# Attention mixed with a Fourier sublayer on one core: keep-warm transposes, first loads, the copy of the sums and the last stores rearranged

## The chip, the cores and the metric

The kernel runs on one core of one Trainium2 chip. A core has a matrix engine (TensorE; PE in the rows below, its weight loads PEld), a vector engine (VectorE, DVE), an activation engine (ScalarE, ACT), a general one (GpSimd, POOL), a queue engine that issues DMAs (SyncE, SP), and 16 DMA engines that all queues share. The metric is device time in microseconds for one execution; lower is better. The kernel before took 1694.63 us, the median of three runs (1694.62, 1694.63 and 1698.86).

## The reference

With x of 2048 rows and 512 columns, the output is `g * a + (1 - g) * b`, where:

```python
g = sigmoid((x * gate_w).sum(-1, keepdims=True))
# a: attention with 32 heads of 16 columns
qkv = (x @ wqkv).reshape(B, S, 3, H, Dh).transpose(2, 0, 3, 1, 4)
scores = einsum("bhqd,bhkd->bhqk", q, k) * Dh ** -0.5
a = einsum("bhqk,bhkd->bhqd", softmax(scores), v).transpose(0, 2, 1, 3).reshape(B, S, D) @ wo
# b: real part of a Fourier transform over columns, then rows
b = dft_seq_re @ (x @ dft_hid_re.T) - dft_seq_im @ (x @ dft_hid_im.T)
```

Everything is float32.

## The kernel before, in words

**Precision.** A float32 product is made of three passes: each operand is split into a high part (a copy in a shorter format) and a low part (the rest), and high·high, high·low and low·high are summed. So a split is one copy on ACT or POOL and one subtraction on DVE or POOL, and a product over 128 rows of contraction is three matmuls. Matmuls use the array in two halves, 64 rows each (j = 0 and 1), that run beside each other.

**The front** (lines 480 to 615). x arrives transposed in 16 tiles (d = 0..3 for the contraction, c = 0..3 for 512 rows of x each), wqkv in column slices. SP issues these loads in program order (lines 500 to 508): for each d the tile x(d, 0) and 256 columns (`near`) of the q weights, then the `near` columns of the k weights, x(·, 1), the other 256 columns (`far`) of q, x(·, 2), `far` of k, x(·, 3). ACT and DVE split each tile (`split`, lines 381 to 383). PE begins with `NWARM = 32` transposes of the identity matrix into scratch banks (`keep_warm`, line 514), whose results nobody reads. Then `project_t` makes its first products: q for f = 0 (columns 0 to 127) on x(·, 0), k for f = 0, q for f = 1 (columns 128 to 255). In the first product every group of three matmuls belongs to one d, and `fillers` puts six more transposes after each of the first three groups. One product is 12 slots, and work such as later splits is handed out by slot number (`after(n, f)`, line 272). `follow` issues the second half-array pass of a product 17 matmuls later (`LAG`).

**Scores, exponentials, values.** For each pair of heads, `score` (line 711) writes a tile of scores into a PSUM bank, ACT takes the exponential (line 693), `pv` (line 723) multiplies by the values and sums over the keys in one bank, `pvb`. Beside the values `pvb` collects the sums of the exponentials, the divisors of the softmax. After 16 steps of keys `pvb` is complete: `quotients` (line 753) copies it to `ob` (ACT, line 758, in this part of the program), four POOL DMAs gather the sums into `lc` (line 761), and `divide` returns three later steps (reciprocal, spread, scaling), which `staged` hands out by the number of the macro step m. `scan` (line 744 on PE, line 746 on DVE) looks for the maxima of heads to come.

**Blocks.** From m = 90 (`SINGLES`) to m = 234 (`OUTM`) two macro steps form a block, whose order of scores (e), scans (c) and spectral products (s, line 969) is written out in `BLOCK_ORDERS`: 80 entries with 24 spectral products per half (the long block), or 56 with 16 (the short one). Both have 16 score tiles. Scores and scans take turns in five PSUM banks: a bank's next matmul has to wait until ACT or DVE has read it. At the end of a block PE does four `pv` steps in a row (32 matmuls in the profile's rows). Every fourth block follows a completed `pvb`: this concerns 18 of the 20 copies of line 758, 12 ahead of long blocks and 6 ahead of short ones. POOL splits the coefficients of the spectral products (lines 253 and 254), one unit per 12 products.

**The end.** After the last `pv`, the last head pair is divided, and the rows 3, 7 to 15 of the output (in tiles of 128 rows) are finished: row 8 first, then 9, 13, 10, 14, 11, 15 on DVE (`take_in`, line 914), and 12, 3, 7 on POOL (line 1182), after products with g on ACT. SP stores 3 and 7 (`store_out(3)`, line 918), then 8, 9, 10, 11; ACT's queue stores 13, 12, 14, 15 (line 1207). A queue issues in order: a store whose row is not finished holds up those behind it.

Of the kernel before, what the change touches and what calls it, by code (L numbers as in the profile page):

```python
# [18 lines left out]
P = 128  # L19
# [4 lines left out]
NP = H // 2  # L24
NB = S // P
ND = D // P
NC = S // 512
# [7 lines left out]
FRONT = 5 * SCANS + 44  # L35
FOLDED = range(FRONT)
FOLD_PACE = 2.05
NWARM = 32
STEPS = NP * PERIODS
MACROS = STEPS // 2  # L40
LAG = 17
# [1 line left out]
SINGLES = 90  # L43
# [16 lines left out]
def build(tc, x, xT, wqkv, wo, wrT, wiT, cr, ci, gate, out):  # L60
    nc = tc.nc
    with ExitStack() as ctx:
# [197 lines left out]
        with ExitStack() as px:  # L260
# [7 lines left out]
            def scan_bank():  # L268
                singles[0] += 1
                return psf.tile([P, 512], F32, tag=f"s{singles[0] % 5}", name="s")  # L270
# [86 lines left out]
                    close(ps)  # L357

            starts, fillers = set(), []

            def products(parts, close):

                ps = product_bank()
                pairs = [(lhs[a], rhs[b]) for lhs, rhs in parts for a, b in ((0, 0), (0, 1), (1, 0))]
                for n, (lhs, rhs) in enumerate(pairs):
                    nc.tensor.matmul(ps, lhs[0:64], rhs[0:64], start=n == 0, stop=False)  # L366
                    issued[0] += 1
                    if n == len(pairs) - 1:
                        ends[ps.name] = issued[0]
                        starts.add(ps.name)  # L370
                        marks[:] = marks[-8:]
                        if pace[0] is None or seen[0] >= FRONT:
                            seen_by(mark(lhs, rhs))
                    behind_.append((ps, lhs, rhs, n == len(pairs) - 1, close))
                    if len(behind_) > LAG:
                        follow()
                    if n % 3 == 2 and fillers:
                        fillers.pop()(6)
                    beside()

            def split(hi, lo, raw, engine):
# [14 lines left out]
            if True:  # L396
# [88 lines left out]
                    return t[d // 2][:, q4[d % 2]]  # L485

                rq, rk = ([quarter(raws[4 + i], d) for d in range(ND)] for i in range(2))
                near, far = slice(0, 256), slice(256, 512)

                def load_x(c):  # L490
                    for d in range(ND):
                        nc.sync.dma_start(quarter(raws[d], c), xT[d * P:(d + 1) * P, q4[c]])

                def load_cols(i, cols):
                    for h in range(2):
                        src = wqkv[2 * h * P:2 * h * P + 2 * P, 512 * i:512 * i + 512]
                        nc.sync.dma_start(raws[4 + i][h].rearrange("p (d m) -> p d m", m=512)[:, :, cols],
                                          src.rearrange("(d p) m -> p d m", p=P)[:, :, cols])

                for d in range(ND):  # L500
                    nc.sync.dma_start(quarter(raws[d], 0), xT[d * P:(d + 1) * P, q4[0]])
                    nc.sync.dma_start(rq[d][:, near], wqkv[d * P:(d + 1) * P, near])
                load_cols(1, near)
                load_x(1)
                load_cols(0, far)
                load_x(2)
                load_cols(1, far)
                load_x(3)
                nc.sync.dma_start(ones_d.rearrange("a (b c) -> (a b) c", c=32), ones)
                gb = ep.tile([P, D], F32, tag="gb", name="gb", bufs=1)  # L510
                after(40, nc.sync.dma_start, gb, gate.to_broadcast([P, D]))

                warm = [scan_bank(), scan_bank()]
                def keep_warm(k):
                    for n in range(k):
                        nc.tensor.transpose(warm[n % 2][:, 0:P], ident, ident)

                keep_warm(NWARM)
                fillers.extend([keep_warm] * 3)
                for d in range(ND):  # L520
                    split_x(d, 0)
                    split_w(wq, d, rq[d], cols=near)
                for d in range(ND):
                    after(1 + 2 * d, split_w, wk, d, rk[d], nc.vector, near)
                    after(84 + 4 * d, split_w, wq, d, rq[d], nc.vector, far)
                    after(124 + 6 * d, split_w, wk, d, rk[d], nc.vector, far)
                    for c, at in zip(range(1, NC), (10, 32, 56)):
                        after(at + 4 * d, split_x, d, c)
                order = [(wq, q_d, 0, 0), (wk, k_d, 0, 0), (wq, q_d, 1, 0)]
                order += [(w, dst, 0, c) for c in range(1, NC) for w, dst in ((wk, k_d), (wq, q_d))]  # L530
# [89 lines left out]
        with ExitStack() as pa:  # L620
# [98 lines left out]
            def pv(step):  # L719
                p, h, kb = step // PERIODS, step % PERIODS // NB, step % NB  # L720
                banks.step()
                for c, j, r in quads:
                    nc.tensor.matmul(pvb[r:r + VC, :], va[:, kb, 2 * p + j, :], es[step][c][0][:, j * 512:j * 512 + 512],  # L723
                                     start=kb == 0, stop=kb == NB - 1, tile_position=(0, r))
                unused.extend(i for e, i in es.pop(step).values())
                exponentials()
                if kb == NB - 1 and step < STEPS - 1:
                    m = step // 2 + 1
                    for n, f in zip((3, 6, 9) if m < SINGLES else (3, 5, 7) if p < NP - 1 else (2, 3, 4), divide(*quotients(p, h))):
                        staged.setdefault(m + n, []).append(f)  # L730

            scans, late, leaving = [FRONT, FRONT], [], []

# [463 lines left out]
            take_in(8, groups[8][0])  # L1197
            for f in [scaled(8, 1)] + add:
                f()
            store_out(3)  # L1200
            for t in (10, 11):
                part(t, 2)
            for t, j in ((9, 0), (9, 1), (10, 0), (10, 1), (11, 0), (11, 1)):
                take_in(t + 4 * j, groups[t][j])
            for j, queue in enumerate((nc.sync, nc.scalar)):
                for t in (9, 8, 10, 11) if j else (8, 9, 10, 11):
                    queue.dma_start(out[(t + 4 * j) * P:(t + 4 * j + 1) * P, :], ys[t + 4 * j])


# [24 lines left out]
```

## Time and profile before

One execution was profiled. It took 1695.7 us; the span from its first to its last instruction is 1693.9 us.

| engine | busy us | share of the span |
|---|---|---|
| PE | 1676.0 | 99% |
| PE weight loads | 1074.2 | 63% |
| ACT | 1298.4 | 77% |
| DVE | 1256.8 | 74% |
| POOL | 706.9 | 42% |

Of the rows of a timeline: start, duration, engine, line of the kernel, operation, output<-inputs, shapes, number of merged instructions, and in brackets how long the engine was idle before and what ended that. A row with x12 stands for 12 instructions in a row. A matmul's record overlaps with the next one's, so starts tell its rate better than durations do. Stores and loads stand under the queue that issues them; when their bytes moved is read from the DMA rows.

### The profile page before, as it was taken

Reading aid. Unit: us, or ns where it says so; the run is one execution under the profiler, and the core shown is the slowest. Engines: PE = TensorE matmul, PEld = TensorE weight load, DVE = VectorE, ACT = ScalarE, POOL = GpSimd, SP = SyncE. Lnnn points to the kernel's source line nnn. Section 1 sums busy time; section 2 is a strip of 40 time slices with the busy share of each in tenths; the row PEclk is TensorE's granted clock in tenths of the full one; section 3 lists DMA queues with packets and bytes.
Section 4 is the critical chain, followed back from the end, with each engine's and each line's share of the span. In section 5 each row is a group of like instructions: output and inputs, shape, how many; then the busy total and the mean of one; then the engine's idle time right before and its main releaser. Section 6 shows DMA issues by size and latency. Waiting matters only on the chain.

```text
span 1693.9 us, 37082 instructions
## 1 busy us (share of the span) xinstructions
PE 1676.0 (99%) x13688; PEld 1074.2 (63%) x13688; DVE 1256.8 (74%) x2352; ACT 1298.4 (77%) x2427; POOL 706.9 (42%) x890
## 2 busy tenths in 40 slices
PE   9999999999999999999999999999999999999997
PEld 7877778833333333777777677666777777666553
DVE  5699899867777777888888888556888888556324
ACT  5589988799999999656666566777556665778884
POOL 0464301454562322454454444444535445445321
PEclk9999999999999999999999999999999999999999
DMA  7665234554442222233332332573332433335512
GB/s 269 228 231 164 73 113 145 179 179 140 127 139 71 65 69 77 64 109 101 86 100 84 100 101 81 153 246 87 117 107 80 127 89 118 104 107 154 159 34 100
DMA packets 140005, 206.61 MB, mean 122 GB/s; under 512 B 58848, under 2 KB 61392, under 8 KB 139824
## 3 DMA queue, kind: packets, MB, share of 16 engines
q1 hardware_dynamic: 97552, 173.76, 33.2%
q0 software_dynamic: 41696, 29.44, 6.6%
q8 instruction: 108, 1.77, 0.4%
q10 hardware_dynamic: 576, 1.05, 0.2%
q14 instruction: 73, 0.60, 0.1%
HBM read 137.89 MB, written 65.81 MB: 120 GB/s over the span
## 4 chain that ended last, share of the span: by engine, by line
PE 94%; DVE 1%; ACT 1%; DMA 1%; issue 1%; DVEq 0%; ACTq 0%
PE pvb L723 28%; PE z L969 24%; PE s L711 17%; PE s L744 9%; PE xy L350 5%; PE s L187 5%; PE xy L366 5%; DMA q_d<-el 0%; ACT fold L191 0%; DVE y L914 0%; DVE fold L193 0%; DMA ks<-kf_d 0%; ACT c L382 0%; ACT xg L553 0%; DVE rb L1186 0%
## 5 line engine op out<-in xcount | busy, mean ns | idle before, releaser
L693 ACT ACTIVATE e<-s 128x512 f32<-128x512 f32 (+1 forms) x1862 | 1012.5, 681 | 244.2 <-PE s L744 184.6
L746 DVE TENSOR_REDUCE mx<-s 128x1 f32<-128x512 f32 x1320 | 870.3, 688 | 282.7 <-PE s L744 186.2
L711 PE MATMUL s<-qs,ks 50*128 50x512 f32 x2040 | 620.8, 418 | 0.0
L969 PE MATMUL z<-b,chi 64*128 64x512 f32 x2060 | 517.5, 392 | 0.0
L723 PE MATMUL pvb<-e,va 128*17 128x512 f32 x4096 | 492.7, 595 | 0.0
L711 PEld LDWEIGHTS s<-qs,ks 50*128 50x128 f32 x2040 | 306.6, 185 | 210.7 <-ACT e L693 153.1
L744 PE MATMUL s<-ks,qs 48*128 48x512 f32 x1320 | 426.8, 400 | 0.7 <-ACT ab L578 0.7
L969 PE MATMUL z<-b,clo 64*128 64x512 f32 x1030 | 338.6, 393 | 0.0
L969 PEld LDWEIGHTS z<-b,chi 64*128 64x128 f32 x2060 | 327.9, 186 | 13.5
L193 DVE CUSTOM_DVE_ANT_0 fold<-s,fold 128x512 f32<-128x512 f32 x364 | 240.0, 689 | 24.3 <-ACT fold L191 7.6
L744 PEld LDWEIGHTS s<-ks,qs 48*128 48x128 f32 x1320 | 227.4, 185 | 35.8 <-issue 18.7
L723 PEld LDWEIGHTS pvb<-e,va 128*17 128x17 f32 x4096 | 92.3, 96 | 242.3 <-issue 237.5
L187 PE MATMUL s<-ks,qs 48*128 48x512 f32 x728 | 234.4, 400 | 1.5 <-ACT fold L191 1.1
L191 ACT ACTIVATE fold<-s 128x512 f32<-128x512 f32 x364 | 200.5, 605 | 28.5 <-PE s L187 27.3
L969 PEld LDWEIGHTS z<-b,clo 64*128 64x128 f32 x1030 | 175.7, 186 | 8.1 <-POOL clo L254 0.4
L254 POOL TENSOR_TENSOR clo<-craw,chi 128x512 fp32r<-128x512 f32 x126 | 161.8, 1284 | 10.4
L761 POOL DMA_DIRECT2D lc<-ob x124 | 62.5, 510 | 248.2 <-ACT ob L758 156.4
L253 POOL CAST chi<-craw 128x512 fp32r<-128x512 f32 x126 | 77.3, 614 | 212.4 <-PE z L969 166.9
L187 PEld LDWEIGHTS s<-ks,qs 48*128 48x128 f32 x728 | 133.6, 184 | 37.8 <-DVE mx L193 12.3
L366 PE MATMUL xy<-w,b 64*128 64x512 f32 x384 | 120.3, 399 | 0.0
L350 PE MATMUL xy<-w,b 64*128 64x512 f32 x384 | 117.0, 393 | 0.0
L914 DVE SCALAR_TENSOR_TENSOR y<-z,g,y 128x512 f32<-128x512 f32 x44 | 32.5, 750 | 75.1 <-PE z L969 70.0
(137 smaller groups left out, 1519.7 us busy)
## 6 DMA issues: line engine op xcount, KB each, us to landing
craw<-cr SPq DMA_DIRECT2D x64, 256.0 KB
craw<-ci SPq DMA_DIRECT2D x64, 256.0 KB
qs<-q_d SPq DMA_DIRECT2D x126, 128.0 KB
ks<-k_d SPq DMA_DIRECT2D x108, 128.0 KB
ab_d<-ab SPq DMA_DIRECT2D x32, 256.0 KB
y_d<-y SPq DMA_DIRECT2D x32, 256.0 KB
b<-bs_d SPq DMA_DIRECT2D x32, 256.0 KB
qs<-q_d SPq DMA_DIRECT2D x126, 64.0 KB
```

What stands on the lines that cost most here:

```text
L187: nc.tensor.matmul(ps, rows.q[qb // 8][b:b + 48, qb % 8 * P:(qb % 8 + 1) * P], rows.k[c // 2][b:b + 48, c % 2 * 512:(c % 2 + 1) * 512], st ...
L191: seen_by(nc.scalar.activation(fold[j], ps, AF.Relu))
L193: seen_by(nc.vector.tensor_tensor_reduce(out=fold[j], in0=ps, in1=fold[j], scale=1.0, scalar=-3.0e38, op0=ALU.add, op1=ALU.max, accum_out= ...
L254: sub(lo, raw, hi.bitcast(F32))
L350: ins = nc.tensor.matmul(ps, lhs[64:P], rhs[64:P], start=False, stop=last)
L366: nc.tensor.matmul(ps, lhs[0:64], rhs[0:64], start=n == 0, stop=False)
L693: nc.scalar.activation(e if j is None else e[:, j * 512:j * 512 + 512], ps, AF.Exp, scale=SCALE)
L711: nc.tensor.matmul(ps, rows.k[kb // 8][b:b + 50, kb % 8 * P:(kb % 8 + 1) * P], rows.q[h][b:b + 50, c * 512:c * 512 + 512], start=True, sto ...
L723: nc.tensor.matmul(pvb[r:r + VC, :], va[:, kb, 2 * p + j, :], es[step][c][0][:, j * 512:j * 512 + 512], start=kb == 0, stop=kb == NB - 1, ...
L744: nc.tensor.matmul(ps, rows.q[qb // 8][b:b + 48, qb % 8 * P:(qb % 8 + 1) * P], rows.k[c // 2][b:b + 48, c % 2 * 512:(c % 2 + 1) * 512], st ...
L746: nc.vector.tensor_reduce(mx[p][:, j, qb, c:c + 1], ps, axis=AX.X, op=ALU.max)
L969: nc.tensor.matmul(ps, pr_.lhs(j), pr_.rhs(j), start=group.count[j] == 1, stop=group.count[j] == group.size)
```

## The change

Four edits.

1. `NWARM` goes from 32 to 20, and the fillers from 6, 6, 6 to 3, 5, 5 transposes.
2. The first weight loads take 128 columns (`near`) in place of 256. The next 128 columns of q (`middle`) are loaded ahead of x(·, 1) and split from slot 9 on; `far` of q is as before; k's remaining 384 columns (`rest`) are one load per half. The splits of x(·, 1) and x(·, 2) move from slots 10 and 32 to 16 and 34.
3. Inside the blocks the copy of `pvb`, with its four POOL DMAs, is issued at the middle of the next block's order in place of its start.
4. The last stores: SP stores rows 8, 9, 3, 10, 7, 11, ACT's queue 12, 13, 14, 15.

```diff
-NWARM = 32
+NWARM = 20
...
-                        fillers.pop()(6)
+                        keep_warm(fillers.pop(0))
...
-                near, far = slice(0, 256), slice(256, 512)
+                near, middle, far, rest = slice(0, 128), slice(128, 256), slice(256, 512), slice(128, 512)
...
                 load_cols(1, near)
+                load_cols(0, middle)
                 load_x(1)
                 load_cols(0, far)
                 load_x(2)
-                load_cols(1, far)
+                load_cols(1, rest)
                 load_x(3)
...
                 keep_warm(NWARM)
-                fillers.extend([keep_warm] * 3)
+                fillers.extend((3, 5, 5))
...
                     after(1 + 2 * d, split_w, wk, d, rk[d], nc.vector, near)
+                    after(9 + 2 * d, split_w, wq, d, rq[d], nc.vector, middle)
                     after(84 + 4 * d, split_w, wq, d, rq[d], nc.vector, far)
-                    after(124 + 6 * d, split_w, wk, d, rk[d], nc.vector, far)
-                    for c, at in zip(range(1, NC), (10, 32, 56)):
+                    after(124 + 6 * d, split_w, wk, d, rk[d], nc.vector, rest)
+                    for c, at in zip(range(1, NC), (16, 34, 56)):
...
                 if kb == NB - 1 and step < STEPS - 1:
                     m = step // 2 + 1
-                    for n, f in zip((3, 6, 9) if m < SINGLES else (3, 5, 7) if p < NP - 1 else (2, 3, 4), divide(*quotients(p, h))):
-                        staged.setdefault(m + n, []).append(f)
+
+                    def begin():
+                        for n, f in zip((3, 6, 9) if m < SINGLES else (3, 5, 7) if p < NP - 1 else (2, 3, 4),
+                                        divide(*quotients(p, h))):
+                            staged.setdefault(m + n, []).append(f)
+
+                    if SINGLES <= m < OUTM:
+                        staged.setdefault(m + 1, []).append(begin)
+                    else:
+                        begin()
...
-            store_out(3)
             for t in (10, 11):
                 part(t, 2)
...
-            for j, queue in enumerate((nc.sync, nc.scalar)):
-                for t in (9, 8, 10, 11) if j else (8, 9, 10, 11):
-                    queue.dma_start(out[(t + 4 * j) * P:(t + 4 * j + 1) * P, :], ys[t + 4 * j])
+            for queue, rows in ((nc.sync, (8, 9, 3, 10, 7, 11)), (nc.scalar, (12, 13, 14, 15))):
+                for t in rows:
+                    queue.dma_start(out[t * P:(t + 1) * P, :], ys[t])
```

**PE at the start.** Before (s is a scratch bank, xy a product; b and w are the split parts of x and of the q weights):

```order
L516 MATMUL s<-ident 128x128 x32
L366 MATMUL xy<-b_223,w_255 128x512
L366 MATMUL xy<-b_224,w_255 128x512
L366 MATMUL xy<-b_223,w_257 128x512
L516 MATMUL s<-ident 128x128 x6
L366 MATMUL xy<-b_225,w_255 128x512
L366 MATMUL xy<-b_226,w_255 128x512
L366 MATMUL xy<-b_225,w_257 128x512
L516 MATMUL s<-ident 128x128 x6
```

And with the change:

```order
L364 MATMUL s<-ident 128x128 x20
L371 MATMUL xy<-b_225,w_257 128x512
L371 MATMUL xy<-b_226,w_257 128x512
L371 MATMUL xy<-b_225,w_259 128x512
L364 MATMUL s<-ident 128x128 x3
L371 MATMUL xy<-b_227,w_257 128x512
L371 MATMUL xy<-b_228,w_257 128x512
L371 MATMUL xy<-b_227,w_259 128x512
L364 MATMUL s<-ident 128x128 x5
```

The products stand as before; 12 transposes are gone ahead of them and 5 between them.

**ACT at the first block with a copy** (e are exponentials; up to here they come with tiles of 1024 columns among them, from here on in tiles of 512). Before:

```order
L693 ACTIVATE e<-s 128x512 x2
L693 ACTIVATE e<-s_10401 128x1024
L693 ACTIVATE e<-s 128x512 x2
L693 ACTIVATE e<-s_10423 128x1024
L693 ACTIVATE e<-s 128x512 x50
L758 COPY ob<-pvb 128x512
L693 ACTIVATE e<-s 128x512 x64
```

And with the change:

```order
L695 ACTIVATE e<-s 128x512 x2
L695 ACTIVATE e<-s_10394 128x1024
L695 ACTIVATE e<-s 128x512 x2
L695 ACTIVATE e<-s_10416 128x1024
L695 ACTIVATE e<-s 128x512 x60
L768 COPY ob<-pvb 128x512
L695 ACTIVATE e<-s 128x512 x64
```

The copy has moved behind ten more exponentials, that is behind 10 of the 16 of the long block that it stood in front of. In the short blocks it moves behind 7 of 16.

**SP at the end** (one y tile holds two neighbouring rows of the output: y_22353 holds 3, y_23453 holds 7, y_23640 holds 8 and 9, y_23700 holds 10 and 11). Before:

```order
L918 DMA out_dram<-y_22353 128x512
L918 DMA out_dram<-y_23453 128x512
L918 DMA out_dram<-y_22353 128x512
L918 DMA out_dram<-y_23453 128x512
L1207 DMA out_dram<-y_23640 128x512 x2
L1207 DMA out_dram<-y_23700 128x512 x2
```

And with the change, where the same tiles are y_22346, y_23446, y_23633 and y_23693:

```order
L928 DMA out_dram<-y_22346 128x512
L928 DMA out_dram<-y_23446 128x512
L1216 DMA out_dram<-y_23633 128x512 x2
L1216 DMA out_dram<-y_22346 128x512
L1216 DMA out_dram<-y_23693 128x512
L1216 DMA out_dram<-y_23446 128x512
L1216 DMA out_dram<-y_23693 128x512
```

The stores of 8 and 9 now stand ahead of those of 3 and 7, and 10 between these two.

More of the change, by code (lines that the diff above doesn't have):

```diff
@@ L359, in build, with keep_warm @@
             starts, fillers = set(), []
+            warm = [scan_bank(), scan_bank()]
+            def keep_warm(k):
+                for n in range(k):
+                    nc.tensor.transpose(warm[n % 2][:, 0:P], ident, ident)
             def products(parts, close):
@@ L511, in build @@
                 after(40, nc.sync.dma_start, gb, gate.to_broadcast([P, D]))
[L513 to L516, printed above, removed]
                 keep_warm(NWARM)
-                fillers.extend([keep_warm] * 3)
+                fillers.extend((3, 5, 5))
                 for d in range(ND):
```

## The prediction

> **What bounds the kernel now.** I read the chain of waits first, then the timelines of the three places that the change touches: the first 14 us, the blocks with a copy, the last 11 us.
>
> ```profile
> PE 1676.0 (99%) x13688; PEld 1074.2 (63%) x13688; DVE 1256.8 (74%) x2352; ACT 1298.4 (77%) x2427; POOL 706.9 (42%) x890
> PE 94%; DVE 1%; ACT 1%; DMA 1%; issue 1%; DVEq 0%; ACTq 0%
> ```
>
> PE carries the chain from the first transpose to the last product. So time taken out of PE's queue at the start shortens the whole, unless something else sets the pace right behind. A delay on ACT costs only what it makes PE wait. The last microseconds, after PE's last product, belong to the stores. The profiled execution took 1695.7 us, 1.8 above its span of 1693.9 and 1.1 above the median of the runs, 1694.63. The three terms below are differences, worked out inside that span; I take their sum off the median.
>
> **Edit 1 and 2, the front.** PE's timeline, then its weight loads for the transposes in two stretches (count, shortest/median/longest in ns, first and last start):
>
> ```profile
> 1.35 6.50 PE L516 MATMUL s<-ident 128*128 128x128 f32 x32 [1.35 <-POOL ident masks.py:199]
> 7.79 0.96 PE L366 MATMUL xy<-b,w 64*128 64x512 f32 x3
> 8.68 0.88 PE L516 MATMUL s<-ident 128*128 128x128 f32 x6
> 9.48 0.96 PE L366 MATMUL xy<-b,w 64*128 64x512 f32 x3
> ...
> 13.71 0.48 PE L366 MATMUL xy<-b,c 64*128 64x512 f32 x1
> ```
>
> ```profile
> L516 PEld LDWEIGHTS s<-ident x27: 182/226/229, 1.4 to 6.7; 128*128 128x128 f32 x27
> ```
>
> ```profile
> L516 PEld LDWEIGHTS s<-ident x21: 138/140/143, 7.3 to 12.6; 128*128 128x128 f32 x21
> ```
>
> 27 transposes start between 1.4 and 6.7, 0.20 to 0.21 us apart with loads of 226 ns; from 7.3 on the loads take 140 ns, and six transposes in 0.88 us are some 0.11 to 0.12 apart. PE runs at about half rate until 7.1 and at full rate after (the granted clock in the rows of the windows is 1.00 all along; the durations tell it). Between the products a group of six fillers takes 9.48 - 8.68 = 0.80, and three matmuls with their change-over 8.68 - 7.79 = 0.89.
>
> With the change the 20 transposes end at about 1.4 + 20 x 0.213 = 5.7. The first group then runs at half rate until 7.1 and ends near 7.3; three fillers (0.80 - 3 x 0.11 = 0.47) bring the second group to 7.8; with five fillers (0.69) the third stands at 9.4, the fourth at 11.0, and the k product starts at 11.8 in place of 13.71. In short: work before the change of rate is done at half rate whatever it is, so each of the 17 transposes is worth its fast price, 17 x 0.11 = **1.9 us**.
>
> This holds if the operands are there. The last one that each needs, and ACT's long idle stretch behind, read from the timelines of DVE and ACT:
>
> ```profile
> 9.64 0.42 DVE L383 TENSOR_TENSOR w<-raws,w 128x256 fp32r<-128x256 f32 x1
> 10.21 1.45 DVE L383 TENSOR_TENSOR c<-raws,c 128x256 fp32r<-128x256 f32 x4
> ```
>
> ```profile
> 18.00 0.59 ACT L455 CAST eh<-xy 128x512 fp32r<-128x512 f32 x1 [4.16 <-PE xy L350]
> ```
>
> ```profile
> 5.00:10.00 5.00, 5.00 (x28) 4.20 (x27) 3.56 (x8) 3.01 (x7) 0.00 (x0) 1.00 0.99 311
> ...
> 30.00:35.00 5.00, 4.66 (x40) 3.88 (x40) 2.73 (x7) 1.78 (x4) 0.58 (x1) 1.00 0.59 216
> ```
>
> Already before, the fourth q operand is split at 10.06 (needed at 11.0) and the k weights at 11.66 (needed at 11.8). From 5 to 10 us the DMA engines are full (the last two columns: share 0.99, 311 GB/s), so bytes set the arrival. With half the columns, 0.5 of the 2.0 MB ahead of the last k weights go away, 1.6 us at 311 GB/s, and the splits shrink. `middle` adds 0.25 MB ahead of x(·, 1), which still arrives after 2.75 MB in place of 3.0. Its eight small splits (DVE's took 0.36 each for 256 columns, ACT's about as much, so at most 1.5 us on each) fit into ACT's 4.16 us of idleness; without that cover they would hold up `eh`, the copy of the first product, and after it the third product's bank. `rest` is 384 columns in place of 256 for a product that stands far later. Moving the x splits by 2 to 6 slots stays ahead of their products at slots 36 and 60. I put these at nothing. Bounds of the term: 1.0 (one operand 0.9 late) to 2.2 (the gate of PE's rate opens earlier, nothing is late).
>
> **Edit 3, the copy.** PE's `pv` rows mark the ends of blocks, first long blocks, then short ones; below them ACT's rows from the same two places:
>
> ```profile
> 758.60 3.63 PE L723 MATMUL pvb<-e,va 128*17 128x512 f32 x32
> ...
> 771.79 3.63 PE L723 MATMUL pvb<-e,va 128*17 128x512 f32 x32
> ...
> 785.13 3.63 PE L723 MATMUL pvb<-e,va 128*17 128x512 f32 x32
> ```
>
> ```profile
> 1111.55 3.63 PE L723 MATMUL pvb<-e,va 128*17 128x512 f32 x32
> 1121.84 3.63 PE L723 MATMUL pvb<-e,va 128*17 128x512 f32 x32
> 1132.19 3.63 PE L723 MATMUL pvb<-e,va 128*17 128x512 f32 x32
> ```
>
> ```profile
> 775.53 0.59 ACT L758 COPY ob<-pvb 128x512 f32<-128x512 f32 x1 [4.38 <-PE pvb L723]
> 776.02 6.13 ACT L693 ACTIVATE e<-s 128x512 f32<-128x512 f32 x12
> 782.45 2.07 ACT L693 ACTIVATE e<-s 128x512 f32<-128x512 f32 x4 [0.30 <-PE s L711]
> 789.28 6.16 ACT L693 ACTIVATE e<-s 128x512 f32<-128x512 f32 x12 [4.77 <-PE s L744]
> 795.62 2.06 ACT L693 ACTIVATE e<-s 128x512 f32<-128x512 f32 x4 [0.18 <-PE s L711]
> ```
>
> ```profile
> 1115.73 8.02 ACT L693 ACTIVATE e<-s 128x512 f32<-128x512 f32 x16 [2.25 <-PE s L711]
> 1125.65 0.59 ACT L758 COPY ob<-pvb 128x512 f32<-128x512 f32 x1 [1.90 <-issue]
> ```
>
> A long block without a copy takes 771.79 - 758.60 = 13.19, the one with it 13.34: 0.15 more. Short ones take 10.29 and 10.35: 0.06 more. Over 12 long and 6 short blocks that is 12 x 0.15 + 6 x 0.06 = 2.2 us, all that this edit can win. It is so little because the copy sits in ACT's idle time under `pv` (4.38 and 1.90 us); the first exponential is late by less than 0.1.
>
> The new place is not idle. The copy holds ACT for 776.02 - 775.53 = 0.49 us. In a long block it follows ten exponentials of a run of 12 back to back; two more are late by 0.49, then the idle 0.18 takes some of it, and the last four are late by 0.31. In a short block all 16 are back to back, and the nine behind the copy are late by 0.49. What waits is the next matmul in the bank that a late exponential holds, and PE's queue behind it. No row of before shows that wait, so bounds: nothing, if five banks cover it, or 0.49 per copy, if PE is held for all of it. Half of what is late seems nearest, since a bank comes round only after four others, and the last banks of a block are not wanted until `pv`, 3.63 us without scores, is over: 0.15 long, 0.25 short. 12 x 0.15 + 6 x 0.25 = 3.3, less the 2.2 saved: **1.1 us lost**, between 2.2 won and 8.8 - 2.2 = 6.6 lost.
>
> The four DMAs of the copy wait on POOL:
>
> ```profile
> L761 POOL DMA_DIRECT2D lc<-ob x124 | 62.5, 510 | 248.2 <-ACT ob L758 156.4
> ```
>
> They hold POOL for 4 x 0.51 = 2.0 us some 5 us later than now. Behind them stands the split of the next coefficient unit, not wanted before a whole unit (half a long block, 6.6 us) has passed, and the reciprocal is two macro steps away; I put that at nothing. If it were not covered, the spectral product itself would start up to 2.0 late.
>
> **Edit 4, the end.** DVE and POOL finish the rows, SP and ACT's queue store them, then the DMA engines in 40 slices of 0.275 us from 1683 to 1694:
>
> ```profile
> 1682.33 4.03 DVE L914 SCALAR_TENSOR_TENSOR y<-s,g,y 128x512 f32<-128x512 f32 x6
> ```
>
> ```profile
> 1682.62 3.73 POOL L1182 TENSOR_TENSOR y<-y,take 128x512 f32<-128x512 f32 x3 [1.82 <-ACT take L1181]
> ```
>
> ```profile
> 1685.15 1.56 SPq L918 DMA_DIRECT2D out_dram<-y  x2
> 1686.80 3.49 SPq L1207 DMA_DIRECT2D out_dram<-y  x4
> ```
>
> ```profile
> 1684.42 2.97 ACTq L1207 DMA_DIRECT2D out_dram<-y  x4
> ```
>
> ```profile
> DMA  0000000069999999999999999999999994000000
> ...
> DMA packets 1440, 2.62 MB, mean 238 GB/s; under 512 B 160, under 2 KB 160, under 8 KB 1440
> ```
>
> The bytes run without a gap from 1685.2 to 1692.2: ten stores, 2.62 MB in 7.0 us, 0.70 each. They start 0.8 after the first issue at 1684.42. Row 8 is finished at 1683.1, but SP waits for row 3, POOL's second sum (1685.1). With the change row 8 is issued at 1683.1, its bytes start at 1683.9, and the rows that follow (9 at 1683.7, 12 at 1683.9, 13 at 1684.4, 10 and 3 at 1685.1, 14 at 1685.7, 7 and 11 at 1686.4, 15 at 1687.0) are each finished before the 0.70 per store reach them. The end moves by 1685.2 - 1683.9 = **1.3 us**; bounds 0.8 (gaps at the start, where one queue feeds the engines) to 1.6.
>
> **Sum:** -1.9 + 1.1 - 1.3 = -2.1; 1694.63 - 2.1 = **1692.5**.
>
> **Rivals.** (a) *Hidden copy*: five banks cover the late exponentials. The 2.2 are won: -1.9 - 2.2 - 1.3 = -5.4, 1689.2. For it: the run of 12 exponentials takes 6.13 us behind a copy and 6.16 without one, so lateness does not pile up. Against: ACT is back to back there, and even 0.1 us of lateness now costs 0.15. (b) *The copy's whole slot reaches PE*, the slower side: in each of the 18 blocks PE waits 0.49 for a bank: 8.8 - 2.2 - 3.2 = +3.4, 1698.0. It is slower than before once a copy costs over (2.2 + 3.2) / 18 = 0.30. For it: 16 exponentials without idle in the short blocks. Against: ACT's idle 0.18 in the long ones. (c) *A DMA swallows the front's gain*:
>
> ```profile
> 48.80 6.64 DMA q_d<-el
> ```
>
> Here the chain runs over a store of 6.64 us, and PE waits. If that store's end stands fixed, the 1.9 is lost: 1694.4. Against: the store is issued by slot, so it moves with PE, and between 30 and 35 us the DMA share is 0.59, room for the shift. (d) *The full rate comes later*: if only products count towards it, 5.7 us of work (1.4 to 7.1) start at 5.8, and full rate comes at 11.5; 4.4 us at half rate cost 2.2: 1694.7. Against: the loads fall from 226 to 140 ns before the first product starts at 7.79. The Trainium skill, page "TensorE: Matmul & The Clock Gate", section "Part 4: PE-mode transpose", says that transposes do not count as activity for the full clock; by that rule (d) would hold, and the rows just named disagree.
>
> **How the numbers follow.** Forecast 0.49, (a) 0.22, (b) 0.12, (c) 0.12, (d) 0.05. The forecast's own range, from its terms' bounds without the rivals', is 1691 to 1694.5. The range for 8 in 10 reaches over most of (a) and to the middle of (b): 1689.4 to 1696.5. A difference of 0.3% is 5.1 us, about what a measurement here tells from none: below 1689.5 lie half of (a) and a tail of the forecast, 0.15; above 1699.7 only (b) with something added, 0.04; within, 0.81.
>
> **What would show it.** The k product's first matmul near 11.8; blocks with a copy near 13.34 and 10.5; bytes of the stores from 1.3 us earlier against PE's last product. The prediction is wrong if a copy's block costs under 0.05 or over 0.4, if the operands of the first product come late, or if the shift of the front is gone by 60 us.

## The result, and the profile after

The change made the kernel slower: 1701.06 us, the median of 10 runs (1699.79 to 1702.49), against 1696.53 for before in the same comparison (10 runs, 1694.33 to 1700.65). The ratio is 1.0024, 95% interval 1.0014 to 1.0035: by the ratio 4.1 us, between 2.4 and 5.9; the medians lie 4.5 apart. A second comparison gave 1.0034 (1.0023 to 1.0044). I had predicted 2.1 us less than before, and a range that ended at 1696.5. Of the 8.6 us between 1701.06 and my 1692.5, 1.9 are the base (1694.63, a median of three, against 1696.53); the rest is the forecast itself.

A run's time goes with its mean granted clock, which is listed to three digits: of 35 runs of before in one comparison, 15 at 0.998 took 1694.7 on average, 11 at 0.997 took 1697.1, 6 at 0.996 took 1699.0. Where a difference below is "at an equal clock", such groups are compared; that leaves out what an edit does to the clock itself.

The profiled execution of the changed kernel has a span of 1700.7, before's 1693.9. Pairing the matmuls of the two by line and order, the changed kernel's stand 2.4 us earlier at 25 us, 0.5 later at 28, 0.3 later at 330, 3.4 later at 352, 6.0 later at 1555, 8.2 later from 1580 on; behind the last one 1.4 come back. So there are five places to read.

**The front.** PE's timeline of the changed kernel (start, duration, engine, line, ...; L371 was L366, L364 was L516):

```profile
1.35 3.88 PE L364 MATMUL s<-ident 128*128 128x128 f32 x20 [1.35 <-POOL ident masks.py:199]
10.67 0.93 PE L371 MATMUL xy<-b,c 64*128 64x512 f32 x3
26.24 0.50 PE L371 MATMUL xy<-b,c 64*128 64x512 f32 x1 [2.58 <-DVE el L461]
```

The k product starts at 10.67 in place of 13.71, better than the forecast 11.8. The surplus is luck: PE's full rate came earlier in this execution. The weight loads of the transposes show it (count, shortest/median/longest in ns, first and last start); the last four of the twenty take 140 to 143 ns:

```profile
L364 PEld LDWEIGHTS s<-ident x17: 141/231/231, 1.4 to 4.5; 128*128 128x128 f32 x17
```

In the traces' record of the granted clock, full rate begins at 4.4 us here and at 7.1 in before; over the fourteen profiles of this case it begins between 4.2 and 7.1. In a second profile of the changed kernel it begins at 6.6, and k starts at 11.57. In two kernels below with 32 transposes it begins at 6.8, and k starts at 13.53 and 13.55.

Then PE stands still for 2.58 us, for DVE's `el`. `el`, the lower part of a product, has two buffers, and the third product needs the first one back, that is, its store has to land. DVE's rows of the first and the third `el`, SyncE's queue, and the store in the chain of waits:

```profile
15.67 0.68 DVE L461 TENSOR_TENSOR el<-xy,eh 128x512 fp32r<-128x512 f32 x1
```

```profile
25.50 0.69 DVE L461 TENSOR_TENSOR el<-xy,eh 128x512 fp32r<-128x512 f32 x1 [3.78 <-DMA q_d<-el]
```

```profile
15.07 2.95 SPq L497 DMA_DIRECT2D raws<-xT  x4
18.14 0.36 SPq L515 DMA_DIRECT2D ones_d<-ones  x1
18.60 0.38 SPq L473 DMA_DIRECT2D q_d<-eh  x1
19.76 0.33 SPq L284 DMA_DIRECT2D gb<-gate  x1
20.85 0.32 SPq L473 DMA_DIRECT2D q_d<-el  x1
```

```profile
20.85 4.55 DMA q_d<-el
```

The first `el` and its store in before:

```profile
18.62 0.69 DVE L456 TENSOR_TENSOR el<-xy,eh 128x512 fp32r<-128x512 f32 x1 [1.73 <-ACT eh L455]
```

```profile
19.95 0.38 SPq L468 DMA_DIRECT2D q_d<-el  x1
```

With the change the first `el` is finished at 16.35, 3.0 us earlier than before. Its store stands in SyncE's queue behind the last loads of x, is issued at 20.85, 0.9 later than before, and lands at 25.4. The windows from 10 to 25 us, changed kernel first (the last three columns: PE's clock, DMA share, GB/s):

```profile
10.00:15.00 5.00, 5.00 (x39) 4.17 (x41) 3.38 (x11) 2.86 (x8) 0.00 (x0) 1.00 0.91 298
15.00:20.00 5.00, 4.97 (x40) 3.55 (x38) 3.42 (x7) 3.16 (x7) 0.00 (x0) 1.00 1.05 387
20.00:25.00 5.00, 3.40 (x25) 2.15 (x25) 1.36 (x3) 2.99 (x6) 0.00 (x0) 1.00 1.06 395
```

```profile
10.00:15.00 5.00, 5.00 (x30) 3.53 (x31) 3.32 (x9) 3.63 (x8) 0.00 (x0) 1.00 1.06 379
15.00:20.00 5.00, 5.00 (x45) 4.33 (x44) 2.41 (x7) 2.00 (x4) 0.00 (x0) 1.00 1.07 374
20.00:25.00 5.00, 4.59 (x41) 4.07 (x39) 2.68 (x6) 2.50 (x6) 0.00 (x0) 1.00 0.83 298
```

Before, the bytes are through by about 24 us; now fewer move from 10 to 15, and the engines are still busy at 25.

**342 to 350 us.** Windows of the changed kernel; before's clock is 1.00 in all of them:

```profile
342.00:344.00 2.00, 1.74 (x7) 0.60 (x11) 1.61 (x3) 2.00 (x4) 0.00 (x0) 0.59 0.49 158
344.00:346.00 2.00, 2.00 (x12) 0.71 (x6) 0.00 (x0) 0.21 (x1) 0.60 (x1) 0.50 0.96 318
346.00:348.00 2.00, 2.00 (x12) 0.27 (x10) 1.29 (x2) 1.97 (x3) 1.84 (x4) 0.50 0.13 49
348.00:350.00 2.00, 2.00 (x14) 0.82 (x14) 0.38 (x1) 0.64 (x2) 1.92 (x3) 0.71 0.49 131
```

PE ran at half rate for 6.8 us (1.6, 2.0, 2.0 and 1.2 of the four windows), which is the 2.9 us lost there. A second profile of the changed kernel does not show it, so it does not come with every execution of the change.

**The blocks with a copy.** The ends of one long and one short block with a copy in the changed kernel (PE's `pv` rows), the short one between two without:

```profile
775.39 3.63 PE L725 MATMUL pvb<-e,va 128*17 128x512 f32 x32
788.75 3.63 PE L725 MATMUL pvb<-e,va 128*17 128x512 f32 x32
```

```profile
1115.80 3.63 PE L725 MATMUL pvb<-e,va 128*17 128x512 f32 x32
1126.08 3.63 PE L725 MATMUL pvb<-e,va 128*17 128x512 f32 x32
1136.79 3.63 PE L725 MATMUL pvb<-e,va 128*17 128x512 f32 x32
1147.05 3.63 PE L725 MATMUL pvb<-e,va 128*17 128x512 f32 x32
```

The long block takes 13.36 (mean of 12: 13.37, before 13.32), the short one 10.71 between neighbours of 10.28 and 10.26 (mean of 6: 10.72, before 10.34). PE's busy column hides why; the weight loads show it. First the copy and the exponentials around it in that short block, then the two weight loads of the changed kernel that wait for an exponential, long block and short block:

```profile
1130.26 3.60 ACT L695 ACTIVATE e<-s 128x512 f32<-128x512 f32 x7 [2.27 <-PE s L713]
1133.72 0.62 ACT L768 COPY ob<-pvb 128x512 f32<-128x512 f32 x1
1134.19 4.58 ACT L695 ACTIVATE e<-s 128x512 f32<-128x512 f32 x9
```

```profile
785.74 0.18 PEld L754 LDWEIGHTS s<-ks,qs 48*128 48x128 f32 x1 [0.28 <-ACT e L695]
```

```profile
1134.89 0.18 PEld L754 LDWEIGHTS s<-ks,qs 48*128 48x128 f32 x1 [0.56 <-ACT e L695]
```

In the short block the weight load stands ready from 1134.33 on, while the first exponential behind the copy still runs: the bank is wanted long before `pv`.

**The last short block.** GpSimd in the changed kernel, then two of the weight loads that wait for it:

```profile
1565.74 2.04 POOL L771 DMA_DIRECT2D lc<-ob  x4 [10.18 <-ACT ob L768]
1567.78 0.63 POOL L835 CAST b<-wor 128x512 fp32r<-128x512 f32 x1
```

```profile
1571.74 0.30 PEld L979 LDWEIGHTS z<-b,b 64*128 64x128 f32 x4 [0.54 <-POOL b L836]
...
1573.64 0.18 PEld L979 LDWEIGHTS z<-b,b 64*128 64x128 f32 x1 [1.16 <-POOL b L836]
```

The same four DMAs in before:

```profile
1555.85 2.04 POOL L761 DMA_DIRECT2D lc<-ob  x4 [6.33 <-ACT ob L758]
```

GpSimd was idle for 10.18 us, waiting for the late copy, with the splits of the output weights (`wor`) queued behind the DMAs. PE needs those splits in the next block.

**The end.** SyncE's and ScalarE's queues of the changed kernel, and PE's last matmul:

```profile
1691.34 5.05 SPq L1216 DMA_DIRECT2D out_dram<-y  x6
```

```profile
1692.18 3.46 ACTq L1216 DMA_DIRECT2D out_dram<-y  x4
```

```profile
1691.51 0.39 PE L219 MATMUL pvb<-b,clo 64*128 64x512 f32 x1
```

From that last matmul's start to the end of the span it is 9.2 us; before 10.6. The first store is issued 0.2 ahead of it, before 1.1 behind it (1684.42 against 1683.28).

### The profile page after: what moved, and what is told of

It reads as the page before. It is cut to its first block, busy times and chain, and to the rows that moved or that the text cites. A ratio compares the mean times of both kernels' runs of the same rounds, so it can differ in the third digit from the quotient of the medians.

```text
span 1700.7 us, 37044 instructions
## 1 busy us (share of the span) xinstructions
PE 1680.3 (99%) x13671; PEld 1074.4 (63%) x13671; DVE 1257.3 (74%) x2356; ACT 1298.4 (76%) x2431; POOL 706.1 (42%) x890
## 4 chain that ended last, share of the span: by engine, by line
PE 94%; DMA 2%; issue 1%; DVE 1%; ACT 1%; SPq 0%; POOL 0%; DVEq 0%; ACTq 0%; POOLq 0%
PE pvb L725 28%; PE z L979 24%; PE s L713 17%; PE s L754 9%; PE xy L350 6%; PE s L187 5%; PE xy L371 5%; DMA q_d<-el 1%; DMA raws<-xT 1%; DVE el L461 0%; DMA qs<-q_d 0%; DVE y L924 0%; POOL xg L554 0%; ACT ob L768 0%; ACT e L695 0%
## 5 line engine op out<-in xcount | busy, mean ns | idle before, releaser
L371 PE MATMUL xy<-w,b 64*128 64x512 f32 x384 | 120.4, 400 | 0.0
```

## Experiments

Unless said otherwise the edits are made to the kernel before. Each time is the median of 7 to 12 runs, with before's own median in the same comparison beside it; the copy in five short blocks was looked at in one profile only.

### One part at a time

**The last stores alone** (edit 4).

```diff
-            store_out(3)
...
+            for queue, rows in ((nc.sync, (8, 9, 3, 10, 7, 11)), (nc.scalar, (12, 13, 14, 15))):
```

> Only the last stores' new order is made. Theory (the parts add): the time from the last pv product to the end shrinks from 11.1 us by about 1.4 and everything ahead of it stays, so the kernel is 1.4 us faster than before, 1693.2 in its profile's terms against 1694.6. Rival (the stores gain only because the rows came later in the changed kernel): under 0.5 us. Second question, the half-rate stretch of 6.8 us that the changed kernel's profile shows from 342.7: if it comes by chance of the execution, some runs here show a mean clock lower by 0.002 and a time longer by 2 to 3 us, as with any of the kernels; if the changed kernel brings it on, none does.

Measured: 1694.21 against 1696.15, ratio 0.9991 (0.9979 to 1.0003), which by itself is not clear of noise. At a clock of 0.998 it is 1693.4 (6 runs) against 1694.7, so 1.4 less. The profiles agree: from the last matmul's start to the end it is 9.2 to 9.6 us in all seven with this edit, 10.6 to 10.9 in all seven without. Four of the 12 runs have a clock of 0.996 or 0.995 and take 1697.8 to 1700.5: a lower clock comes without the rest of the change.

**The copy alone** (edit 3, all 18 places).

```diff
+                    if SINGLES <= m < OUTM:
+                        staged.setdefault(m + 1, []).append(begin)
+                    else:
+                        begin()
```

> Only the copy of the sums is moved to mid-block, at all 18 places. Theory (the parts add): +0.04 in each of 12 long blocks, +0.4 in each of 5 short ones, +0.4 and 1.8 in the last short one with the splits of the output weights behind the copy's four DMAs on GpSimd: 0.5 + 2.4 + 1.8 = 4.7 us slower than before, with long blocks of 13.37 and short ones of 10.7. Rival 1 (the loss hangs on the shift of the front, that is on where the blocks stand): under 2 us slower. Rival 2 (the two at the last block come from the stores' edit or the front): 2.9 us slower and no wait of PE for GpSimd near 1572.

Measured: 1701.70 against 1696.15, ratio 1.0030 (1.0020 to 1.0040): 5.1 us, and 5.5 at a clock of 0.998. Short blocks with a copy take 10.72, long ones 13.38. The whole loss of the change, and more, is in this edit; the first theory holds.

**The front alone** (edits 1 and 2), and **the transposes alone** (edit 1, loads and splits as before).

```diff
-NWARM = 32
+NWARM = 20
...
-                fillers.extend([keep_warm] * 3)
+                fillers.extend((3, 5, 5))
```

> Only the front is changed: 20 transposes ahead, 3, 5 and 5 between, first loads of 128 weight columns. Theory (the gain is made by 12 us and lost again at the first wait for the store of a lower part, near 26 us): the matmuls from 30 us on stand 0.3 to 0.6 us later than before, although the k product starts 2 to 3 us earlier; time within 0.7 us of before. Rival (what was lost in the front belongs to the interplay with the copy or to one execution): matmuls stand 1.9 us earlier from 30 us to the end, and the kernel is 1.9 us faster.

> Only the transposes are cut, to 20 in front and 3, 5 and 5 between; the loads and splits stay as before. Theory 1 (the smaller loads of 128 columns hold up the later loads and with them the store that the lower part's buffer waits for): without them the gain of some 1.9 us is still there at 30 us, and the kernel is 1 to 2 us faster than before. Theory 2 (the store is bound to the end of the input loads, which PE does not move): the k product starts up to 1.9 us earlier but PE waits that much longer at the first waits up to 26 us; matmuls at 30 us stand within 0.3 us of before, and the time is the same. Theory 3 (the first operands come too late for PE): PE waits for the split q or k weights in the first 14 us, and the k product starts within 0.5 us of 13.71.

Measured: the front alone 1698.74 against 1696.15, ratio 1.0014 (1.0004 to 1.0023). By the medians that is 2.6 us more than before, at a clock of 0.997 0.9 more. The rest goes with the clock: none of its 12 runs is above 0.997, against 16 of before's 35, and its profile shows half rate from 26.0 to 29.4 us, where PE's wait of 2.45 us ends. The transposes alone take 1695.30, ratio 0.9995 (0.9983 to 1.0007), no difference; at a clock of 0.998 it is 0.4 more (8 and 15 runs). In the profile of the latter matmuls stand 2.1 us earlier at 18 and at 24 us (part of that is again the clock: full rate from 5.6 us, before from 7.1), 0.5 at 28, and none at 62. Two waits take the gain. PE's row and DVE's of the first:

```profile
25.23 0.49 PE L372 MATMUL xy<-b,c 64*128 64x512 f32 x1 [1.30 <-DVE el L462]
```

```profile
24.48 0.69 DVE L462 TENSOR_TENSOR el<-xy,eh 128x512 fp32r<-128x512 f32 x1 [2.49 <-DMA q_d<-el]
```

DVE's idle time ahead of all its `el` up to 62 us, summed by what ended it (us, times), first before, then this kernel:

```profile
  DMA q_d<-el: 3.5, 1
```

```profile
  DMA q_d<-el: 8.6, 3
```

PE's first wait, near 25 us, takes 1.2 to 2.6 us in all five profiles with 20 transposes and separate buffers, and at most 0.25 in all seven with 32. The second, near 55 to 59, comes and goes: in the seven with 32 it is between nothing and 2.5. So theory 2 of the transposes is right: PE comes earlier, the store hardly does (issued at 19.19 against 19.95). The loads of 128 columns cost about 1.4 on top (1698.0 against 1696.6 at a clock of 0.997, 5 and 3 runs). By 15 us the three profiles with these loads have moved 3.7 MB, before and the transposes alone 4.3 (from the windows' GB/s). Whether it is their shorter rows or their order was not separated.

### Where the copy's cost lies

**The copy moved in the last short block only**, and **in the other five short blocks only**.

```diff
-                    if SINGLES <= m < OUTM:
+                    if m == OUTM - 2:
```

> The copy is moved to mid-block only in the last of its 18 blocks, the short one behind which GpSimd splits the output weights. Theory (the four DMAs of the copy, issued some 8 us later on GpSimd, push the splits behind them, and PE's products of the output part wait for those splits): that block and the next together take 2.2 us longer than before, PE waits 1.5 to 2 us for GpSimd near 1565, and the kernel is 2 us slower than before. Rival (those waits came from earlier lateness that had added up by then): that block takes 0.4 longer, PE waits there less than 0.5, and the time is within 0.7 us of before.

```diff
-                    if SINGLES <= m < OUTM:
+                    if SINGLES <= m < OUTM and BLOCKS[(m - SINGLES) // 2] == 16 and m < OUTM - 2:
```

> The copy is moved to mid-block only in the other five short blocks. Theory 1 (PE waits for the exponential behind the copy, once, for the 0.49 us that the copy holds ScalarE): a short block with a copy takes 10.7 against 10.3 without, each shows one weight load that waits 0.5 us for an exponential, and the blocks behind them are not longer; 5 x 0.4 = 2.0 us in all, none of it in the long blocks. Theory 2 (the later DMAs on GpSimd make the split of the next coefficients late): the longer block is the one behind the copy, and what waits is a product of the spectral part.

Measured, the last alone: `pv` rows and one of the waits of the block behind:

```profile
1548.44 3.63 PE L723 MATMUL pvb<-e,va 128*17 128x512 f32 x32
1559.15 1.91 PE L723 MATMUL pvb<-e,va 128*17 128x512 f32 x16
1566.02 1.91 PE L723 MATMUL pvb<-e,va 128*17 128x512 f32 x16
```

```profile
1564.91 0.18 PEld L976 LDWEIGHTS z<-b,b 64*128 64x128 f32 x1 [1.17 <-POOL b L833]
```

10.71 and 6.87, where before has 10.32 and 5.09: 2.2 us at one place. The medians lie 0.4 apart (1697.28 against 1696.86, ratio 1.0001, 0.9991 to 1.0010), but these runs happened to have a higher clock than before's (0.9978 against 0.9970 on average); at 0.998 it is 1697.0 (8 runs) against 1695.2 (12), 1.9 more. The other five, in one profile: 10.72 on average, neighbours 10.29, the last block with its copy at the start 10.29, long blocks with a copy 13.32 as before. The theory of the first and theory 1 of the second hold.

### What takes the front's gain

**Another queue**: transposes and last stores as in the change, and the stores of the first three products on GpSimd's queue.

```diff
-                    project_t(w, dst, f, c)
+                    project_t(w, dst, f, c, nc.gpsimd if n < 3 else nc.sync)
```

> Against before: 20 transposes in front and 3, 5 and 5 between, the last stores in the changed order, and the stores of the first three products go through GpSimd's queue in place of SyncE's, so that they don't stand behind the input loads. Theory (PE's wait near 26 us is for a lower part's buffer whose store stands behind the loads): the first store lands by 23 us, the wait of 1.3 us at 25.23 is gone, and matmuls at 30 to 50 us stand 1.5 to 2 us earlier than before; a second wait for such a store at 52 to 59 us may still take it back. Rival (the DMA engines are full until 25 us whatever the queue): the store lands at 25 us as now and nothing changes against the kernel with fewer transposes alone. With the stores of the end, 1.4 us, the time is 1.4 to 3.4 us below before.

Measured: 1695.25 against 1696.86, ratio 0.9990 (0.9981 to 0.9999): no more than the last stores bring; at a clock of 0.998 it is even 0.3 more than before (7 and 12 runs). GpSimd's row of the store, and DVE's of the wait:

```profile
17.05 0.55 POOL L474 DMA_DIRECT2D q_d<-el  x1
```

```profile
23.82 0.69 DVE L462 TENSOR_TENSOR el<-xy,eh 128x512 fp32r<-128x512 f32 x1 [2.32 <-DMA q_d<-el]
```

The store is issued 2.1 us earlier than with the transposes alone (19.19) and lands 0.7 earlier. The rival is right in the main: with the DMA engines full (share 1.06 from 20 to 22 us), 2.1 us at the issue became 0.7 at the landing.

**Common buffers**: transposes and last stores as in the change; `eh` (three buffers) and `el` (two) become five that both take in turn. The bytes are the same, but a buffer comes back after five parts, and the third product's lower part waits for an upper part's store.

```diff
-                        hi = ep.tile([P, 512], F32R, tag="eh", name="eh", bufs=3)
-                        lo = ep.tile([P, 512], F32R, tag="el", name="el")
+                        hi = ep.tile([P, 512], F32R, tag="eh", name="eh", bufs=5)
+                        lo = ep.tile([P, 512], F32R, tag="eh", name="el", bufs=5)
```

> Against before: fewer transposes (20, then 3, 5 and 5), the last stores in the changed order, and the upper and lower parts of a projected product take turns in five common buffers in place of three and two of their own, so that the lower part of the third product waits for the store of the first upper part, issued 1.5 us ahead of the first lower part's. Theory (the front's gain is lost because the lower part's buffer waits for a store that the full DMA engines hold back to 25 us): the wait at 25.23 shrinks by 0.5 to 1.5 us, and so does the one near 59; matmuls at 70 us stand 0.5 to 1.5 earlier than before, and the time is 2 to 3 us below before. Rival (whatever the buffer, the same full DMA engines hold PE until 25 and 58 us): the waits stay, and with the stores' 1.4 the time is 1.4 below before.

Measured: 1691.15 against 1695.27, ratio 0.9974 (0.9963 to 0.9985): 4.1 us less by the medians, more than the 2 to 3 expected. DVE's idle time ahead of `el` is now:

```profile
  DMA q_d<-eh: 1.6, 1
```

against 8.6 us, and PE's wait of 1.30 shrinks to 0.39. Matmuls stand 3.4 us earlier at 75 us than in before.

**Common buffers alone**, with before's transposes and stores.

> Against before: only the five common buffers for upper and lower parts; the 32 transposes in front and three times 6 between stay, and the last stores too. Theory 1 (the buffers let the gain of the fewer transposes through, which was 2.1 us until 18 us and nothing at 59): alone they win only what PE waited for these stores in before, some 0.5 us near 25 and 1 us near 56, so matmuls at 70 us stand 1 to 1.5 us earlier than in before, and the other 2 of the 3.4 us come from the transposes. Theory 2 (the buffers do it all, and the transposes are worth nothing): matmuls at 70 us stand 3 us or more earlier, and the kernel is 3 us faster.

Measured: 1694.30 against 1696.23, ratio 0.9988 (0.9979 to 0.9998); at a clock of 0.998 it is 0.9 less (10 and 8 runs), and matmuls stand 2.0 earlier at 75 us. With the stores' 1.4 that leaves 1.6 of the 3.9 that the kernel above wins at that clock: the transposes' gain, once nothing behind them waits. The times at an equal clock speak for theory 1; the ratio's interval reaches 3.6 us and does not exclude theory 2. The sizes are rough, since the profile of before itself stands 1.2 to 2.0 later at 75 us than three others with the same front, so one profile's position tells no more than that.

### The clock

**Five transposes near 341**, where PE is idle for 0.71 us in before, with the last stores as in the change.

```diff
                 run_due(True)
+                ps = product_bank()
+                for n in range(5):
+                    nc.tensor.transpose(ps[:, 0:P], ident, ident)
```

> Against before: the last stores in the changed order, and five transposes on PE where it is idle for 0.71 us near 341, ahead of the scores of the next part. Theory (a step of the clock, 3.4 us, goes to half rate when PE was idle in the step before it, and the idle 0.7 us at 341 is the commonest cause of the runs that are 2 to 5 us longer): half-rate steps near 342 become rare, 10 or more of 12 runs show a mean clock of 0.998 or 0.999, and the median falls by 1 to 2 us against the kernel with the stores alone, to 2.5 to 3.5 below before. Rival (the half-rate steps come whatever PE does): the same mixture of clocks as in before, and 1.4 below before.

Measured: 1694.50 against 1696.86, ratio 0.9986 (0.9977 to 0.9995). None of 12 runs has a mean clock of 0.996 or less (before: 8 of 29), four have 0.997. I had expected at most two of these, and a median 1 to 2 below the stores alone; it lies 2.4 below before where theirs lay 1.9, and at a clock of 0.998 1.2 below, about what the stores alone bring. The direction agrees, the size is left open.

**The same transposes with the common buffers**, and **the changed kernel again**, in one comparison with the common buffers.

> The kernel with the common buffers, and five transposes where PE is idle near 341. Theory: if half-rate steps of the clock follow PE's idle time, no run has a mean clock of 0.996 or less, and the median is 0.5 to 1.5 below the same kernel without these transposes. Rival (the transposes do nothing to the clock): the two have the same mixture of clocks and the same median.

> The changed kernel itself once more, on one chip with the two that follow. Theory (the parts add, each as it was measured alone: stores -1.4, copy +5.2, front +0.5 to +0.9 at an equal clock): 4.3 to 4.7 us slower than before among runs of an equal mean clock. If the longer wait near 23 to 26 us makes half-rate steps of the clock commoner, as the kernel with the front alone suggests (mean clock 0.9963 against 0.9972 in before), the medians lie 6 to 7 apart and the mean clock is lower than in before; if it does not, the medians lie 4.5 apart as in the first comparison.

Measured: 1690.89 against 1695.27, ratio 0.9971 (0.9960 to 0.9982), the lowest median here; all seven runs at 0.998 or 0.999. But the common buffers without these transposes have only one of seven below 0.998, and the medians lie 0.3 apart, less than expected: with PE's waits in the front gone there is little left to show. The changed kernel took 1700.96, ratio 1.0034, 5.4 more than before at a clock of 0.998. The parts at an equal clock make -1.4 + 5.5 + 0.9 = 5.0: they add, to 0.4. On the clock the run decides little: its runs have 0.9973 on average against 0.9978, and the medians lie 5.7 apart, between the two cases set against each other.

## Why the prediction was wrong, by its steps

**The front, forecast -1.9, measured +0.9 at an equal clock and +2.6 by the medians.** The price of a transpose was right: between profiles whose full rate began at about the same time the k product starts 1.5 to 2.0 us earlier, and 1.6 stay where nothing waits. But the forecast of 11.8 was worked out with 7.1 us as the start of full rate, and that start moves from one execution to the next: the 10.67 of the k product, and part of the 2.1 won by 18 us, are luck.

The step that failed is "I put these at nothing", and with it the reason given against rival (c): "the store is issued by slot, so it moves with PE". It does not move with PE. The first lower part was finished 3.0 us earlier and its store was issued 0.9 later, behind the loads in SyncE's queue; then it took 4.55 us to land, with the DMA engines full (share 1.06 from 20 to 25 us). I had looked at the store of 48.80 and at the room between 30 and 35 us, and not asked when the first store lands, at the end of some 20 us of full DMA engines. Two buffers of `el` had covered it, since PE came there late enough; in the profile of the stores alone, with before's front and full rate from 4.2 us, the third `el` waits for that store as well, and matmuls lose 0.5 us. The bounds, 1.0 to 2.2 gained, held no loss, though I had the figure beside them (0.99, 311 GB/s) that said the engines were full. The narrower loads were put at nothing too: x(·, 1) stood behind fewer bytes, but fewer had moved (3.7 MB against 4.3 by 15 us), and these loads cost about 1.4.

**The copy, forecast +1.1, measured +5.5.** The long blocks are right: 0.05 more than before each, where I had the 0.15 lost cancel the 0.15 saved. The short blocks are the first wrong size: 0.25 against a plain block, measured 0.43, so rival (b), the whole 0.49, was near. The reason, "a bank comes round only after four others", fails because ScalarE has no idle time left: with 16 exponentials in a row each bank is wanted as soon as it is read. Six blocks cost 6 x 0.38 = 2.3 more than before, where I had 6 x 0.19 = 1.1. The second is "I put that at nothing" for GpSimd's DMAs. I had the right price for it, "up to 2.0 late", and looked behind the DMAs in an ordinary block only, where it holds. In the last block other splits stand behind them, and one place costs 1.8 (2.2 less the 0.4 of its block). By the blocks the sum is 12 x 0.05 + 2.3 + 1.8 = 4.7; 0.8 of the 5.5 stays unplaced, within what these groups of runs can tell.

**The last stores, forecast -1.3, measured -1.4.** Right, mechanism and size.

**The rivals.** (b) and (c) had 0.12 each and both came true in part, (b) in the six short blocks. I had treated them as exclusive, so no case held both and the range ended at 1696.5. Two of the signs of being wrong that I had named appeared: a short block's copy cost over 0.4, and the shift of the front was gone by 60 us. (d), that the transposes would not bring the full rate, is refuted again: 20 transposes in 3.88 us, with weight loads of 231 and then 141 ns, mean that the rate doubled during them, before a product had run (the first at 5.17). The Trainium skill says in "TensorE: Matmul & The Clock Gate", section "Part 4: PE-mode transpose", that it would not; the row decides.

## What to carry to other kernels

An engine that is made to arrive earlier gains only up to its next wait for something that doesn't move with it; in a stretch where the DMA engines are full, ask for every buffer when its store is issued and when it lands, not when its contents are ready. A small operation moved into an engine's run of back-to-back work costs the engine that waits nearly its whole length where no idle time follows (0.43 of 0.49 us in the short blocks; in the long ones, where some idle time of ScalarE follows, 13.37 against 13.20 without a copy, so 0.17), and its followers on other queues must be looked up at every place where it runs, the last above all. Here the cure was a sharing of five buffers that cost no memory: it let the gain of the fewer transposes through.

## What the runs showed of the hardware

PE's granted clock drops to one half for steps of 3.4 us in the middle of a kernel. By that, an estimate, one step costs 1.7 us of full rate and 0.001 of the mean clock. Of the profiles with such a stretch it stands at 26 to 29 us in two, at 56 to 63 in three, at 342 to 352 in three, always right behind a place where PE was idle. The kernel with the copy alone shows two of them; its windows at 55 us:

```profile
55.00:58.00 3.00, 0.60 (x6) 0.51 (x8) 0.76 (x2) 0.00 (x0) 2.47 (x6) 1.00 1.00 335
58.00:61.00 3.00, 3.00 (x18) 2.38 (x16) 0.69 (x1) 0.58 (x1) 0.00 (x0) 0.50 0.52 171
```

An idle time of 0.71 us stood right ahead of the two steps at 342 in the changed kernel's first profile, and 0.70 at the same place was followed by none in its second. PE's rows of the two, first and second profile:

```profile
342.26 0.74 PE L754 MATMUL s<-ks,qs 48*128 48x512 f32 x1 [0.71 <-ACT ab L580]
```

```profile
342.67 0.50 PE L754 MATMUL s<-ks,qs 48*128 48x512 f32 x1 [0.70 <-ACT ab L580]
```

The Trainium skill (page "TensorE: Matmul & The Clock Gate", section "Part 1: The HAM clock gate") describes a free-running activity window of 3413 ns, which fits the length of the steps and that they differ between executions. Its section "Why this matters for your kernels" puts the gap that matters at about 3 us; here far shorter ones were followed by half rate. About half of before's runs (48 of 97 with a listed clock) were at 0.997 or less, so a median of three runs can miss by 2 us. What decides between the two rows above was not settled.
